# Turning k and q through the first layer's banks in halves, with layer steps given out slot by slot

## The chip, the cores and the metric

The kernel runs on one core of a Trainium2 chip. The metric is the device time of one execution in microseconds (us). In what follows PE is the matmul engine, DVE the vector engine, ACT the scalar engine, POOL the GpSimd engine, and SP the queue from which nearly all transfers are issued.

## What is computed

A thresholded attention is followed by a two-layer network with a shrinking non-linearity. The reference, cut to what matters:

```python
def _attn_ref(q, k, v, tau):                       # 8 batches, 8 heads, 576 rows, 64 columns
    scores = np.matmul(q, k.transpose(0, 1, 3, 2)) / np.sqrt(q.shape[-1])
    thresh = np.max(scores, axis=-1, keepdims=True) - tau
    scores = np.where(scores >= thresh, scores, -1000000000.0)
    scores = scores - np.max(scores, axis=-1, keepdims=True)
    attn = np.exp(scores)
    attn = attn / (np.sum(attn, axis=-1, keepdims=True) + 1e-09)
    return np.matmul(attn, v)

def _moe_ref(x, w_in, w_out):                      # x: 4608 x 512, w_in: 512 x 2048
    h = x @ w_in
    g = h - np.tanh(h)
    return g @ w_out
```

The attention's output, its heads laid side by side, is the network's x.

## The kernel before, in words

**Pairs and tiles.** The 64 heads are taken as 32 pairs, numbered from 0. A pair has nine tiles of 128 query rows (`TPP = 9`): four of each head, and one that holds the last 64 rows of both, the shared tile. Four pairs (`HPAIR`) make a batch. There are 288 tiles.

**Slots.** The order of all work is written out by hand, in a loop over slots `s` from -8 to 292 (line 709). All engines work their instructions in the order in which this loop emits them. In slot `s` it emits, in this order: `shift` (line 347, the row maximum for a pair of tiles, `nb`, in every second slot), `scores(s + 8)`, `kink(s + 5)` on ACT (line 360), `bend` (tanh of the hidden block of the slot before, line 511), `weights(s)` (exp, line 404, in odd slots), the layer steps that the slot is given, `shrink` (line 514, on DVE: `g`, the hidden block less its tanh), stores, `attend(s - 2)` (line 409, tiles in twos, so in odd slots), `norm` (line 450, on DVE), `emit_x` (line 470), and then what `plan` holds for the slot: loads, splits and turns. In a slot where a pair ends in a shared tile and the next begins with one, no scores are emitted and in the next slot two tiles.

**Scores.** `scores` (line 308) multiplies q with k in two fp16 halves, a high and a low one that `split` (line 186, on POOL) makes. Needed for it are `qT` and `kT`, the transposed halves, and `kS`, which is `kT` with its 64-row halves exchanged. DVE evacuates a score tile from PSUM (line 341) and takes the row maximum with it. ACT's `kink` then makes z. For pairs from the seventh on, a DMA transposes z to zT, and ACT takes exp of it.

**Turns.** `turn(p, t)` (line 248) makes `kT` or `qT` of pair `p`: nine transposes on PE into one PSUM tile of 128 x 1152 fp16, one copy by DVE into SBUF, and for k two copies by POOL that make `kS`. For q of pairs from 8 on a DMA does it, except for every fourth pair (`q_by_dma`, line 244). A turn stands in the slot `TPP * p - 8 - d`, with d from `PREP` and the lines below it: for k, d is 3 for even and 6 for odd pairs from the sixth pair on.

**PSUM.** `ps_big` has two buffers of two banks each; score tiles take them in turn, and the turns of k and q take one too (tag "big", line 257). `ps_h` has two buffers of one bank (tag "h"): hidden blocks psH (line 502), and psX, the transposed attention output of a pair (line 472). A hidden block's bank is free once `shrink` has read it, which is emitted one slot after its matmuls. `ps_y` and `ps_o` have one bank each.

**Layers.** For batch m there are 16 h steps (`hidden`, four matmuls of 512 columns, line 498) and 16 y steps (`project`, four such matmuls, line 524; after the fourth of a row block DVE copies psY out). `layers(m, tail)` (line 559) puts both in a list. The slot loop starts a new list every 36 slots from slot 40 on (line 711): stage m is slots 40 + 36m to 75 + 36m. It gives out the list at a rate, `share` steps for each slot of `room`; the slots in which k is turned (`turns`) are left out of `room`. In stages 1 to 5 this gives one step to each of 32 slots, h and y mostly by turns. What is left at the end runs after the last slot.

Below, the position of a slot is s modulo 36. Before, k is turned at positions 7, 13, 25 and 31, q on PE at position 26.

Of the kernel before, what the change touches and what calls it, by code (L numbers as in the profile page):

```python
# [11 lines left out]
FP16 = mybir.dt.float16  # L12
# [6 lines left out]
def kernel(  # L19
# [11 lines left out]
    nc = tc.nc  # L31
    P = 128
# [13 lines left out]
    HPAIR = H // 2  # L46
    NPAIR = B * HPAIR
# [4 lines left out]
    TPP = 9  # L52
    NTILE = NPAIR * TPP
# [7 lines left out]
    W = 2 * S  # L61

    AHEAD = 8
# [62 lines left out]
    ps_big = pool("ps_big", 2, space=PSUM)  # L126
    ps_o = pool("ps_o", 1, space=PSUM)
    ps_h = pool("ps_h", 2, space=PSUM)
# [107 lines left out]
    def turn_chunk(out, c, lhsT):  # L236
        rhs = ident_f16
        if c == 4:
            out, rhs = in_heads(out), by_head(rhs)
        nc.tensor.matmul(  # L240
            out=out, lhsT=lhsT, rhs=rhs, is_transpose=True, start=True, stop=True
        )

    def q_by_dma(p):

        return p >= 2 * HPAIR and p % 4 != 0

    def turn(p, t):
        hl = hls.pop((p, t))
        if t == "q" and q_by_dma(p):  # L250
            m = mats[p, t] = qk_pool.tile([P, W], FP16, name=f"{t}T", tag=t)
            nc.sync.dma_start_transpose(
                out=m.rearrange("p (c r) -> p c r", c=TPP),
                in_=hl.rearrange("p c a d -> p (c a d)"),
            )
            return
        ps = ps_big.tile([P, W], FP16, name=f"ps_{t}", tag="big")
        for c in range(TPP):
            turn_chunk(
                ps[:, c * P : (c + 1) * P], c, hl[:, c, :, :].rearrange("p a d -> p (a d)")  # L260
            )
        m = qk_pool.tile([P, W], FP16, name=f"{t}T", tag=t)
        nc.vector.tensor_copy(out=m, in_=ps)
        mats[p, t] = m
        if t == "k":
            sw = qk_pool.tile([P, W], FP16, name="kS", tag="ks")
            for lo, hi in ((0, D), (D, 0)):
                o, i = sw[lo : lo + D, :], m[hi : hi + D, :]
                nc.gpsimd.tensor_copy(out=o, in_=i)  # L269
            mats[p, "ks"] = sw  # L270
# [27 lines left out]
    def kind(i):  # L298

        return "AB"[i % 2]  # L300

    def place(i):

        p, j = divmod(i, TPP)
        j = j - p % 2
        return (p, None, 4) if j in (-1, 8) else (p, j // 4, j % 4)
# [243 lines left out]
                    )  # L550


    EARLY = lambda m: 3 if m else 3
    LAST = 1

    FIRST = 3
    quarters = lambda m: [(m, ms, part) for ms in range(4) for part in range(4)]

    def layers(m, tail):


        def h_step(n):
            if tail and n % 2:
                ps = ps_big.tile([P, MB], F32, name="psHt", tag="big")
            else:
                ps = ps_h.tile([P, MB], F32, name="psH", tag="h")
            hidden(m, n, ps)

        def y_step(m, ms, part):
            if part == 0:  # L570

                odd = tail and (m, ms) > (B - 2, 1) and ms % 2 == 0
                pl, tag = (ps_o, "o") if odd else (ps_y, "y")
                ys[m, ms] = pl.tile([P, d_model], F32, name="psY", tag=tag), odd
            ps, odd = ys[m, ms]
            project(m, ms, part, ps, odd)

        def y_half(h):

            n = d_model // 2  # L580
            pl, tag = ((ps_y, "y"), (ps_o, "o"))[h]
            ps = pl.tile([P, n], F32, name="psY", tag=tag)
            for part in range(4):
                project(m, 3, part, ps, h == 0, slice(h * n, h * n + n))

        now = quarters(m - 1)[EARLY(m - 1) :] if m > 0 else []
        if m < NMB - 1:
            now += quarters(m)[: EARLY(m)]
        else:
            now += quarters(m)[:12]  # L590
        n = 16 + len(now)


        ahead = n - max(0, EARLY(m) - 3) - LAST if m < NMB - 1 else n - 9 - LAST
        steps, at, i = [], [], 0

        def ready(y):
            last = 4 * y[2] + 3
            return y[0] < m or len(at) > (last if m else 15) and at[last] + 2 < i

        while now or len(at) < 16:
            if len(at) < 16 and (
                not now or not ready(now[0]) or len(at) * ahead <= i * 16
            ) and not (m == B - 1 and i < FIRST):
                steps.append(lambda a=len(at): h_step(a))
                at.append(i)
            elif ready(now[0]):
                steps.append(lambda y=now.pop(0): y_step(*y))
            else:
                steps.append(lambda: None)  # L610
            i += 1
        if m == NMB - 1:
            steps += [lambda h=h: y_half(h) for h in range(2)]
        return steps

    ys = {}


    def w_pieces():
# [39 lines left out]
    for p in range(1, NPAIR):  # L659
        first = TPP * p - AHEAD  # L660
        for d, f in PREP[3 if p == 1 else 0 :]:
            d -= p == 1 and d in (3, 5)
            if d in (7, 8) and q_by_dma(p):
                d = d + 2
            if p in (2, 4):
                d = {8: 9, 7: 8, 5: 6}.get(d, d)
            elif d == 5 and p >= 5:
                d = 6 if p % 2 else 3
            plan.setdefault(first - d, []).append(lambda p=p, f=f: f(p))
        d = 7 if q_by_dma(p) else 3 - (p == 1 or p >= 5)  # L670
        d = 4 if p in (2, 4) else d
        plan.setdefault(first - d, []).append(lambda p=p: turn(p, "q"))
# [15 lines left out]
    todo, stage = [], 0  # L688
# [5 lines left out]

    turns = set()
    for p in range(HPAIR + 1, NPAIR):
        d = 6 if p % 2 else 3
        turns.add(TPP * p - AHEAD - (d if p >= 5 else 5))  # L700

    kinks, wts, atts = {}, {}, {}
    for i in range(NTILE + 3):
        at = i - 4 if i < HPAIR * TPP else i
# [4 lines left out]
    for s in range(-AHEAD, NTILE + LAG + 3):  # L709
        p, j = divmod(max(s, 0), TPP)  # L710
        if 0 <= s < NTILE and j == 2 + LAG and p % HPAIR == 0 and p >= HPAIR:
            assert not todo
            todo = layers(stage, False)
            room = range(s, min(s + HPAIR * TPP, NTILE))
            if room[-1] + 1 < NTILE:
                room = [a for a in room if a not in turns]
            share = len(todo) / len(room)
            done, stage = 0.0, stage + 1
        if s == NTILE:
            todo = layers(stage, True)  # L720
            share, done, stage = 1, 0.0, stage + 1
        if 0 <= s + AHEAD - 1 < NTILE:
            shift(s + AHEAD - 1)

        n = s + AHEAD
        if 0 < n < NTILE and place(n)[1] is None and kind(n) == "B":
            scores(n - 1)
        if 0 <= n < NTILE and (place(n)[1] is not None or kind(n) == "B"):
            scores(n)
        if s == 1 - AHEAD:  # L730
            for t in ("k", "q", "ks"):
                turn_first(t, 1)
        for i in kinks.pop(s, []):
            kink(i)
        bend()
        for i in wts.pop(s, []):
            weights(i)
        if 0 <= s < NTILE + FIRST:
            if todo and (s >= NTILE or s in room):
                done += share  # L740
                if s < NTILE and s == room[-1]:
                    done = 1e9
                while todo and done >= 1:
                    todo.pop(0)()
                    done -= 1
        if s == 0:
            nc.vector.tensor_tensor(
                out=fold, in0=ident_bf[:, 0:64], in1=ident_bf[:, 64:P], op=ALU.add
            )
        shrink()  # L750
        for store in stores[:-1]:
            store()
        del stores[:-1]
        for i in atts.pop(s, []):
            pp, jj = divmod(i, TPP)
            if i < NTILE:
                attend(i)
                odd = pp % 2
                if jj == 3 + odd:
                    norm(pp, 0)  # L760
                elif odd and jj in (0, 8):
                    norm(pp - (jj == 0), 1)
            if pp and jj == 1 + pp % 2:
                emit_x(pp - 1)
        for step in plan.pop(s, []):
            step()
        if s + AHEAD in cast_when:
            w_cast()
        if s + AHEAD in load_when:
            w_load(next(pieces))  # L770

    for step in todo:
        step()
        bend()
        shrink()
        for store in stores:
            store()
        stores.clear()
# [10 lines left out]
    _ = bass_utils  # L789
# [35 lines left out]
```

## Time and profile before

| | |
|---|---|
| median of 3 runs | 531.08 us (531.07 to 531.32) |
| profiled execution | 532.69 us |
| its span, first to last instruction | 530.9 us |
| granted PE clock | full (1.00) |
| first score of slot 40, 76, 112 (stages 0, 1, 2) | 64.56, 116.20, 178.93 us |
| first score of slot 148, 184, 220, 256 (stages 3 to 6) | 237.59, 295.49, 352.92, 410.45 us |

The rest, from about 455 us on, is layer work alone. Lines of the profile name a source line, the engine, the operation, the tile written and the tiles read. In the order of time, the first number is the start in us from the span's start and the second the busy time; "x4" says that four such instructions are merged, and a bracket at the end tells how long the engine was idle before it and who ended the wait. In the list of waits the numbers are the sum in us, how many times, and the longest one. Matmuls overlap, and their ends are modelled, so a PE busy time is longer than the distance to the next start.

### The profile page before, as it was taken

Reading aid. Unit: us, or ns where it says so; the run is one execution under the profiler, and the core shown is the slowest. Engines: PE = TensorE matmul, PEld = TensorE weight load, DVE = VectorE, ACT = ScalarE, POOL = GpSimd, SP = SyncE. Lnnn points to the kernel's source line nnn. Section 1 sums busy time; section 2 is a strip of 40 time slices with the busy share of each in tenths; the row PEclk is TensorE's granted clock in tenths of the full one; section 3 lists DMA queues with packets and bytes.
Section 4 is the critical chain, followed back from the end, with each engine's and each line's share of the span. In section 5 each row is a group of like instructions: output and inputs, shape, how many; then the busy total and the mean of one; then the engine's idle time right before and its main releaser. Section 6 shows DMA issues by size and latency. Waiting matters only on the chain.

```text
span 530.9 us, 12707 instructions
## 1 busy us (share of the span) xinstructions
PE 507.7 (96%) x4606; PEld 286.4 (54%) x4606; DVE 422.1 (80%) x1179; ACT 433.4 (82%) x617; POOL 289.3 (54%) x390
## 2 busy tenths in 40 slices
PE   8999899989999989999999999999999999999996
PEld 4666566554555545555555555555555555444444
DVE  5999889997898878998889888888899887554440
ACT  5999999998898989988998989899998989544330
POOL 7999999684738366574738383846657430000000
PEclk9999999999999999999999999999999999999999
DMA  7843668989799999899998999999988976400113
GB/s 215 242 141 112 216 214 168 184 145 201 180 199 162 183 181 202 167 193 205 180 198 180 199 175 216 157 198 185 204 169 196 202 133 110 105 36 25 39 41 80
DMA packets 208607, 86.79 MB, mean 163 GB/s; under 512 B 176160, under 2 KB 200992, under 8 KB 208544
## 3 DMA queue, kind: packets, MB, share of 16 engines
q1 hardware_dynamic: 207952, 85.56, 77.4%
q8 instruction: 36, 0.59, 0.5%
q10 hardware_dynamic: 592, 0.43, 0.3%
q14 instruction: 27, 0.22, 0.1%
HBM read 36.70 MB, written 9.44 MB: 87 GB/s over the span
## 4 chain that ended last, share of the span: by engine, by line
PE 48%; issue 13%; ACT 12%; DVE 12%; POOL 7%; DMA 7%; SPq 1%; ACTq 0%; POOLq 0%; DVEq 0%
PE psY L524 15%; PE psH L498 12%; PE psS L331 9%; ACT z L368 5%; DVE sc L341 4%; ACT pT L396 3%; DMA zT<-z 3%; PE psHt L498 3%; DVE g L517 2%; PE psO L432 2%; ACT th L511 2%; POOL kS L269 2%; ACT pT L404 2%; DMA vraw<-in_v_dram 2%; PE psS L322 2%
## 5 line engine op out<-in xcount | busy, mean ns | idle before, releaser
L341 DVE TENSOR_SCALAR_CACHE_REDUCE sc<-psS 128x576 f32<-128x576 f32 x288 | 212.9, 753 | 34.2 <-PE psS L331 21.3
L368 ACT ACTIVATE z<-sc,nb 128x576 bf16<-128x576 f32 x288 | 216.0, 769 | 27.6 <-DVE nb L353 27.1
L524 PE MATMUL psY<-w_out_sb,g 128*128 128x512 bf16 (+1 forms) x592 | 146.0, 374 | 0.8 <-DVE yo L537 0.8
L404 ACT ACTIVATE pT<-zT 128x1152 f16<-128x1152 bf16 x117 | 135.0, 1154 | 10.6 <-DMA zT<-z 10.4
L269 POOL COPY kS<-kT 64x1152 f16<-64x1152 f16 x62 | 70.8, 1142 | 125.4 <-DVE nb L353 123.7
L498 PE MATMUL psH<-xT,w_in_sb 128*128 128x512 bf16 x480 | 123.3, 379 | 0.7 <-DVE g L517 0.3
L331 PEld LDWEIGHTS <-qT 128*128 128x128 f16 x1024 | 75.1, 97 | 67.3 <-issue 11.8
L331 PE MATMUL psS<-kT,qT 128*128 128x512 f16 (+1 forms) x512 | 104.3, 285 | 7.2 <-DVE sc L341 4.0
L517 DVE SCALAR_TENSOR_TENSOR g<-th,psH 128x512 bf16<-128x512 f32 x128 | 87.6, 684 | 25.5 <-ACT th L511 23.6
L331 PE MATMUL psS<-kS,qT 128*128 128x512 f16 x496 | 101.3, 286 | 1.7 <-POOL kS L269 1.6
L511 ACT ACTIVATE th<-psH 128x512 f32<-128x512 f32 x128 | 74.6, 583 | 21.9 <-PE psH L498 21.8
L524 PEld LDWEIGHTS <-g 128*128 128x128 bf16 x592 | 51.0, 98 | 57.2 <-issue 3.5
L498 PEld LDWEIGHTS <-w_in_sb 128*128 128x128 bf16 x576 | 48.8, 98 | 53.2 <-issue 1.0
L432 PE MATMUL psO<-vb,pT 128*128 128x65 bf16 x1024 | 53.3, 194 | 0.0
L432 PEld LDWEIGHTS <-pT 128*128 128x128 f16 x1024 | 44.2, 98 | 9.4
L193 POOL TENSOR_TENSOR khl<-kraw,khl 128x576 f16<-128x576 f32 x31 | 39.7, 1281 | 2.6
L193 POOL TENSOR_TENSOR qhl<-qraw,qhl 128x576 f16<-128x576 f32 x31 | 39.7, 1280 | 2.6
L396 ACT ACTIVATE pT<-psZ 128x512 f16<-128x512 bf16 (+1 forms) x54 | 35.1, 654 | 2.6 <-PE psZ L387 2.1
L537 DVE COPY yo<-psY 128x512 f32<-128x512 f32 (+1 forms) x31 | 21.1, 682 | 13.6 <-PE psY L524 12.4
L458 DVE TENSOR_TENSOR osb<-psO,rc 128x256 bf16<-128x256 f32 x64 | 27.2, 424 | 2.2
L425 PE MATMUL psO<-vb,pT 128*128 128x130 bf16 x128 | 28.1, 220 | 0.6 <-DVE nb L353 0.6
L387 PE MATMUL psZ<-ident_bf,z 128*128 128x128 bf16 x243 | 22.5, 220 | 2.1 <-ACT pT L396 1.3
(79 smaller groups left out, 509.5 us busy)
## 6 DMA issues: line engine op xcount, KB each, us to landing
vraw<-in_v_dram SPq DMA_DIRECT2D x32, 256.0 KB, 3.6
out_dram<-yo SPq DMA_DIRECT2D x32, 256.0 KB, 3.1
kraw<-in_k_dram SPq DMA_DIRECT2D x31, 256.0 KB, 3.1
qraw<-in_q_dram SPq DMA_DIRECT2D x31, 256.0 KB, 3.4
wt<-in_moe_w_in_dram SPq DMA_DIRECT2D x8, 512.0 KB, 4.6
wt<-in_moe_w_out_dram SPq DMA_DIRECT2D x8, 512.0 KB, 4.2
zT<-z SPq DMA_TRANSPOSE x117, 3.7
qraw<-in_q_dram SPq DMA_DIRECT2D x32, 32.0 KB, 3.1
```

Of the source, the lines that this page charges most:

```text
L193: nc.gpsimd.tensor_tensor(out=hl[:, :, 1, :], in0=x, in1=hl[:, :, 0, :], op=ALU.subtract)
L269: nc.gpsimd.tensor_copy(out=o, in_=i)
L331: nc.tensor.matmul(out=ps[:, dst], lhsT=lhs, rhs=kk[:, src], start=(n == 0), stop=(n == 1),)
L341: nc.vector.tensor_scalar(out=sc, in0=ps[:, lo : lo + S], scalar1=SC, scalar2=None, op0=ALU.mult, op1=ALU.max, accum_out=mx[:, c : c + 1],)
L368: nc.scalar.activation(out=z, in_=sc, func=ACT.Prelu, bias=nb, scale=1.0, alpha=STEEP)
L396: nc.scalar.activation(out=pt[:, off * P : (off + n) * P], in_=ps[:, 0 : n * P], func=ACT.Exp)
L404: nc.scalar.activation(out=pt[:, 0 : n * P], in_=zts.pop(i)[:, 0:n, :], func=ACT.Exp)
L432: nc.tensor.matmul(out=po[:, t - 1 + ab, :], lhsT=pt[:, blk * P : (blk + 1) * P], rhs=vb[:, hh, c, :], start=False, stop=(n == 7), skip_gr ...
L498: nc.tensor.matmul(out=ps, lhsT=w_in_sb[:, c, n * P : (n + 1) * P], rhs=xs[m][:, c, :] if m < B else xR[:, c, :, :], start=(c == 0), stop= ...
L511: nc.scalar.activation(out=th, in_=ps, func=ACT.Tanh)
L517: nc.vector.scalar_tensor_tensor(out=gs[m][:, n, :], in0=th, scalar=-1.0, in1=ps, op0=ALU.mult, op1=ALU.add,)
L524: nc.tensor.matmul(out=ps, lhsT=gs[m][:, n, ms * P : (ms + 1) * P], rhs=w_out_sb[:, n, cols], start=(n == 0), stop=(n == DF_C - 1),)
```

## The change

From the seventh pair on (`BYHALF = HPAIR + 2`, p from 6), `turn` no longer takes a score buffer. It turns five chunks into one `ps_h` bank and copies them, then four chunks into a `ps_h` bank and copies those. k is turned at d = 4 for even and d = 5 for odd pairs (`k_lead`): one slot earlier for even pairs, one later for odd ones, so at positions 6, 14, 24 and 32. Layer steps of the stages before the tail are no longer given out at a rate: `layers` gets the list of slots without a k turn and gives each step a slot. It prefers an h step when h steps are due by a count, and a y step where it can be run and the next slot is a turn's slot or no h step is due.

In stages 1 to 5 the h steps then stand at positions 4, 7, 9, 11, 12, 15, 17, 18, 20, 22, 25, 26, 28, 29, 33 and 34, and the y steps in the other slots that aren't a turn's: 1, 2, 3, 5, 8, 10, 13, 16, 19, 21, 23, 27, 30, 31, 35 and 0. Before, the h steps stood at 4, 6, 9, 11, 14, 16, 18, 20, 22, 24, 27, 29, 32, 34, 0 and 2. No instruction is added or taken away on PE; on DVE, each turn from the seventh pair on has two copies in place of one.

```diff
+    BYHALF = HPAIR + 2
+
+    def k_lead(p):
+        if p < BYHALF:
+            return 6 if p in (2, 4) or p == HPAIR + 1 else 5 - (p == 1)
+        return 5 if p % 2 else 4
+
...
-        ps = ps_big.tile([P, W], FP16, name=f"ps_{t}", tag="big")
-        for c in range(TPP):
-            turn_chunk(
-                ps[:, c * P : (c + 1) * P], c, hl[:, c, :, :].rearrange("p a d -> p (a d)")
-            )
         m = qk_pool.tile([P, W], FP16, name=f"{t}T", tag=t)
-        nc.vector.tensor_copy(out=m, in_=ps)
+        if p < BYHALF:
+            spans, pl, tag = ((0, TPP),), ps_big, "big"
+        else:
+            spans, pl, tag = ((0, 5), (5, TPP)), ps_h, "h"
+        for c0, c1 in spans:
+            n = (c1 - c0) * P
+            ps = pl.tile([P, n], FP16, name=f"ps_{t}", tag=tag)
+            for c in range(c0, c1):
+                turn_chunk(
+                    ps[:, (c - c0) * P : (c - c0 + 1) * P], c,
+                    hl[:, c, :, :].rearrange("p a d -> p (a d)"),
+                )
+            nc.vector.tensor_copy(out=m[:, c0 * P : c1 * P], in_=ps)
         mats[p, t] = m
...
-    EARLY = lambda m: 3 if m else 3
+    EARLY = lambda m: 3
...
-    def layers(m, tail):
+    def layers(m, tail, slots=None):
...
+        if slots is not None:
+            for nth, i in enumerate(slots):
+                spare = len(slots) - nth - (16 - len(at)) - len(now)
+                can = now and ready(now[0]) and (m or i >= CAST_BY[now[0][2]])
+                due = len(at) * (len(slots) - OWN(m)) <= nth * 16
+                lull = i + 1 not in slots and spare >= 0
+                if len(at) < 16 and not (can and (lull or not due)) and (due or spare <= 0):
+                    steps.append((i, lambda a=len(at): h_step(a)))
+                    at.append(i)
+                elif can:
+                    steps.append((i, lambda y=now.pop(0): y_step(*y)))
+            assert len(at) == 16 and all(ready(y) for y in now)
+            steps += [(i, lambda y=y: y_step(*y)) for y in now]
+            return steps
...
+    CAST_BY = (56, 56, 58, 64)
+    OWN = lambda m: EARLY(m) + 2
...
-            d -= p == 1 and d in (3, 5)
+            d -= p == 1 and d == 3
             if d in (7, 8) and q_by_dma(p):
                 d = d + 2
-            if p in (2, 4):
-                d = {8: 9, 7: 8, 5: 6}.get(d, d)
-            elif d == 5 and p >= 5:
-                d = 6 if p % 2 else 3
+            if d == 5:
+                d = k_lead(p)
+            elif p in (2, 4):
+                d = {8: 9, 7: 8}.get(d, d)
             plan.setdefault(first - d, []).append(lambda p=p, f=f: f(p))
...
-    turns = set()
-    for p in range(HPAIR + 1, NPAIR):
-        d = 6 if p % 2 else 3
-        turns.add(TPP * p - AHEAD - (d if p >= 5 else 5))
+    turns = {TPP * p - AHEAD - k_lead(p) for p in range(HPAIR + 1, NPAIR)}
...
-            todo = layers(stage, False)
             room = range(s, min(s + HPAIR * TPP, NTILE))
-            if room[-1] + 1 < NTILE:
-                room = [a for a in room if a not in turns]
-            share = len(todo) / len(room)
-            done, stage = 0.0, stage + 1
+            todo = layers(stage, False, [a for a in room if a not in turns])
+            stage += 1
         if s == NTILE:
-            todo = layers(stage, True)
-            share, done, stage = 1, 0.0, stage + 1
+            todo = [(s + n, step) for n, step in enumerate(layers(stage, True))]
+            stage += 1
...
-        if 0 <= s < NTILE + FIRST:
-            if todo and (s >= NTILE or s in room):
-                done += share
-                if s < NTILE and s == room[-1]:
-                    done = 1e9
-                while todo and done >= 1:
-                    todo.pop(0)()
-                    done -= 1
+        while todo and todo[0][0] <= s < NTILE + FIRST:
+            todo.pop(0)[1]()
```

More of the change, by code (lines that the diff above doesn't have):

```diff
@@ L770 @@
             w_load(next(pieces))
-    for step in todo:
+    for _, step in todo:
         step()
```

## The prediction, made before the changed kernel ran

> **What bounds the kernel now.** I read the page first, then the list of waits, then the order of time around single turns, and last the groups by form.
>
> ```profile
> PE 507.7 (96%) x4606; PEld 286.4 (54%) x4606; DVE 422.1 (80%) x1179; ACT 433.4 (82%) x617; POOL 289.3 (54%) x390
> ...
> PE   8999899989999989999999999999999999999996
> ```
>
> PE is busy throughout, but busy time of overlapping matmuls says little, so I took the rhythm from the starts: in the order of time four 512-column matmuls of a layer step take 0.86 us, an ordinary score tile 0.49, an attend group 0.31, a shared one 0.29, an x turn 0.25, nine transposes 0.50. A stage of 36 slots holds 32 layer steps (27.6), 32 ordinary score tiles (15.6), two pairs of shared ones at 1.11 (2.2), 16 attends (5.0), 4 shared ones (1.2), 4 x turns (1.0) and 5 turns of k and q (2.5): 55.1 us. By the starts of slots 112, 148, 184, 220 and 256 (178.93, 237.59, 295.49, 352.92, 410.45) a stage takes 58.7, 57.9, 57.4 and 57.5. PE thus stands still about 2.8 us a stage; a PE wait added there counts fully, and no more than that can be won. Who ends its waits:
>
> ```profile
> PE psS L331 <- DVE sc L341: 4.0, 7, 1.2
> ...
> PE ps_k L240 <- DVE sc L341: 1.9, 11, 0.2
> ...
> PE psS L331 <- POOL kS L269: 1.6, 5, 0.3
> ```
>
> These hang on the k turn: it takes a score buffer, so it waits for a score's evacuation, the next score waits in turn, and kS arrives late. One such turn (slots 150 to 154):
>
> ```profile
> 241.11 0.68 DVE L517 SCALAR_TENSOR_TENSOR g<-th,psH 128x512 bf16<-128x512 f32 x1
> ...
> 242.32 0.75 DVE L341 TENSOR_SCALAR_CACHE_REDUCE sc<-psS 128x576 f32<-128x576 f32 x1
> ...
> 242.99 0.76 DVE L341 TENSOR_SCALAR_CACHE_REDUCE sc<-psS 128x576 f32<-128x576 f32 x1
> 243.13 0.66 PE L240 MATMUL ps_k<-ident_f,khl 128*128 128x128 f16 x9 [0.18 <-DVE sc L341]
> ...
> 243.79 0.69 DVE L517 SCALAR_TENSOR_TENSOR g<-th,psH 128x512 bf16<-128x512 f32 x1
> 243.81 0.41 PE L331 MATMUL psS<-kT,qT 128*128 128x512 f16 x2
> ...
> 244.40 0.75 DVE L263 COPY kT<-ps_k 128x1152 f16<-128x1152 f16 x1
> ...
> 247.59 0.41 PE L331 MATMUL psS<-kS,qT 128*128 128x512 f16 x2 [0.32 <-POOL kS L269]
> ```
>
> The reader should see: the turn starts 0.06 after the first sc ends (242.32 + 0.75), 0.33 late by PE's rhythm; the next score is 0.18 late; the copy waits behind an sc and a g on DVE and harms nobody; at 247.59 PE is late for kS by 0.49 (the row before started at 246.86; two matmuls of it take 0.24). That is 1.0 us for this turn.
>
> **What the skill says.** "Perfetto Trace Analysis", Tensor Engine Instruction: only weight loads are pulled ahead on PE, and ACT, DVE and GpSimd are strict FIFO. The copy above agrees: transposes over at 243.8, copy at 244.40 behind g. The same page, Identifying the Most-Contended Engine: recurring bubbles on a saturated engine can mean too few PSUM buffers; here 0.33 and 0.18 recur every second k turn. "PSUM — Partial Sum Buffer", Terms: eight banks of 2 KiB. The program's tiles use them all (two psS of two banks, two "h", one "y", one "o"), so the halves have to share "h" with psH and psX. No trace row shows banks.
>
> **The change, part by part.** Positions are slots modulo 36; stage 3 (slots 148 to 183) stands for stages 1 to 5.
>
> (1) Removed: waits on a score bank. By PE's rhythm this is 0.51 each at positions 7 and 25; kS adds 0.49 at 7, and the score behind the q turn at 26 is 0.23 late. At 13 the score after the turn waited 1.41, 0.63, 0.17 and 0 in four stages (196.29 and 254.18 are two of these rows; tanh is late behind a late zT; mean 0.55), at 31 nothing. About 2.3 a stage, of the 2.8.
>
> (2) Added on DVE: two copies for one.
>
> ```profile
> L263 DVE COPY kT<-ps_k 128x1152 f16<-128x1152 f16 x31 | 23.3, 751 | 1.1 <-PE ps_k L240 0.9
> ...
> L488 DVE COPY xT<-psX 128x512 bf16<-128x512 bf16 x32 | 13.4, 420 | 1.8 <-PE psX L481 1.8
> ...
> L291 DVE COPY kT<-ps_k 128x640 f16<-128x640 f16 x1 | 0.5, 491 | 0.9 <-PE ps_k L240 0.9
> ```
>
> 491 + 420 - 751 = 160 ns a turn, 33 turns: 5.3 us, in DVE's 20% of idle time; by itself nothing.
>
> (3) Added: waits on "h" banks. In the changed program every k turn stands at positions 6, 14, 24 or 32, on a slot without attend, and the next slot (7, 15, 25, 33) always carries an H step, whose psH takes the bank of the first half. So H waits for the first copy, and behind H stand all later scores and attends. PE reaches H 0.49 + 0.50 + 0.49 = 1.48 after the turn's slot began. DVE takes that slot's sc first, at best 0.69 after the slot's start (239.64 against 238.95 in slot 149), goes on 0.67 later (242.32, 242.99), copies 0.49 and frees the bank 0.06 later: 1.91. No k turn costs less than 0.43. With what DVE has before it:
> - Position 6: PE work up to slot 150 is as before. First half 241.11 to 241.39; the second needs the bank of H148, whose g ends at 241.79: wait 0.46. H is due at 242.56, its bank free at 242.99 + 0.49 + 0.06 = 243.54: 0.98. Together 1.44, for 1.00.
> - Position 14: the x copies of slot 157 end about 2.9 after that slot's start, sc runs from 2.97, copy 3.64 to 4.13; H is due at 3.68: 0.5, plus what late tanhs leave, 0.25. 0.75, for 0.55.
> - Position 24: slot 168 starts at 269.75. Without the output copy that before has in slot 167 (269.63), g ends near 270.26, normalization and nb take 0.55, sc 270.80, copy 271.47 to 271.96; H is due at 271.23 and starts at 272.02: 0.79.
> - Position 32: x copies as at 14, no late g: 0.51, for nothing.
>
> (4) The q turn at position 26 (pairs 12, 16, ... 28; likewise 7 and 8) keeps its H step in the same slot, and that psH isn't read before the next slot. So both halves get the same bank. From the H at 272.02: + 0.86 + 0.31 is slot 170 at 273.19; + 0.49 + 0.86 is 274.54. The first half needs the bank of H169, whose g comes after sc(170) (273.88) on DVE: 274.55 to 275.24, wait 0.76. The second half needs the first's copy: 275.30 + 0.45, + 0.49, + 0.06 = 276.30, wait 0.72. Slot 171 starts near 276.52, for 275.07 in this row of before:
>
> ```profile
> 274.34 0.66 PE L240 MATMUL ps_q<-ident_f,qhl 128*128 128x128 f16 x9
> ...
> 275.04 0.76 DVE L263 COPY qT<-ps_q 128x1152 f16<-128x1152 f16 x1
> 275.07 0.41 PE L331 MATMUL psS<-kT,qT 128*128 128x512 f16 x2
> ```
>
> Positions 24 to 26 lose 1.45 net.
>
> (5) Layer steps keep their number in each stage; H steps now come in pairs of slots (11 and 12, 17 and 18, 25 and 26, 28 and 29, 33 and 34). ACT has 10% idle in these stages and DVE about 12% (26.5 of 30 us): I take 0, bounds -0.5 and +1 a stage. psY's last part at position 0 is followed by the next psY at position 1; position 0 has no score and two shared ones (1.11) stand between, so the 0.69 copy is hidden. Even k turns now come a slot earlier, odd ones a slot later; khl is long there (for pair 6 at 65.4, turn near 67.6), and kS moves ahead of split_v on POOL, which idles 8.7 us before such copies. DMAs keep their number; stores shift by single slots on SP. All 0. After the last score (455 us on) the order is the same.
>
> Sum for a stage: 0.45 + 0.2 + 1.45 + 0.5 = +2.6; five stages +13.0. Stage 0: four k turns at about 1.0 and two q turns at 1.4, less 2.2 of old waits, is +4.6; ACT is the fuller engine there (28.1 of 30 us), so half: +2.3. Stage 6: pair 30 +1.2, pair 31 +0.75, together +2. In all +17.3 on a span of 530.9, which with what lies around it was 532.69; the median of the runs, 531.08, is 1.6 lower. On that median: 548.4, I say **548**.
>
> **Rivals.**
> - Only the unavoidable waits: DVE has no backlog at the turns. Four k turns at 0.51 and q at 1.48 are 3.5 for 2.3: +1.2 a stage, 6.0, with 1.2 for stages 0 and 6: **538**. For it: a PE that stalls lets DVE catch up. Against: normalization, output copy and x copies stand just before three of the four turns.
> - Waits pile up: DVE waited 51 times, 36.1 us, for tanh, 0.7 each; if half of 33 turns meet one, 0.5 x 33 x 0.7 = 11.6 more: **560**.
> - Faster: freed score buffers are all that counts. If the copies return banks before H is due, 2.3 x 5 + 2 goes and q costs 1.2 a stage: 531 - 13.5 + 6 = **523**. It decides once the new waits average under 2.3 / 5 = 0.46 a turn. Against it is the floor in (3), 0.43 for k, and 1.48 for q.
> - No net change: **531**, when (3) and (1) happen to cancel.
>
> **How the numbers follow.** Forecast (541 to 556) 0.60, unavoidable waits only 0.18, piling up 0.11, faster 0.08, none 0.03. The range 535 to 559 leaves out faster, none and the upper part of piling up. Differences under 0.2% (1.1 us) can't be told from none: faster 0.08, same 0.03, slower 0.89.
>
> **What would show it.** Right: new waits of PE at psH L513 and ps_k/ps_q L240 on DVE's kT and qT copies and g; psS no longer waiting for kS; two q halves about 1 us apart; stages near 60.5. Wrong: psH starts without a gap after turns (faster), or PE waits for sc or ACT for zT grow instead (another cause).

## The result, and the profile after

The changed kernel takes 553.19 us (median of 4 runs, 551.92 to 554.34), against 531.2 for the kernel before on the same chip: a ratio of 1.0413, with a 95% interval of 1.0386 to 1.0439. It is slower. The profiled span is 552.1 us, against 530.9.

The page shows that the work on PE is the same and the span is longer. This is the row of busy time, in us and as a share of the span, with the number of instructions:

```profile
PE 509.5 (92%) x4606; PEld 286.4 (52%) x4606; DVE 424.5 (77%) x1213; ACT 435.9 (79%) x617; POOL 290.5 (53%) x390
```

PE has the same 4606 matmuls, 1.8 us more busy time, and 92% where it had 96%. Its idle time, span less busy time, rose from 23.2 to 42.6 us, which is 19.4 of the 21.2 us that the span grew; so nearly all of the loss is time in which PE stands still. The 34 more instructions on DVE are the second copies of the 34 turns. By form, the copies of k and q sum to 38.3 us for 33.1 before.

The time from the first score of one stage to that of the next, from the starts in the order of time:

| stage | 0 | 1 | 2 | 3 | 4 | 5 | from slot 256 to the end |
|---|---|---|---|---|---|---|---|
| before | 54.9 | 59.5 | 58.7 | 57.9 | 57.4 | 57.5 | 120.5 |
| after | 59.0 | 62.7 | 61.2 | 60.5 | 60.1 | 60.1 | 123.7 |
| difference | 4.1 | 3.2 | 2.5 | 2.6 | 2.7 | 2.5 | 3.2 |

(The table ahead of the prediction gives 116.20 us for slot 76. That is the start of slot 74; slot 76 starts at 119.47. No step of the prediction used it.)

Whom PE waits for, from the list of waits of the changed kernel (sum in us, how many, the longest):

```profile
PE psH L513 <- DVE kT L278: 10.4, 22, 0.8
...
PE ps_k L240 <- DVE g L532: 7.1, 11, 1.6
...
PE ps_q L240 <- DVE g L532: 4.5, 6, 1.0
PE ps_q L240 <- DVE qT L278: 4.1, 7, 0.6
...
PE psY L539 <- DVE yo L552: 1.6, 2, 0.8
...
PE psS L346 <- DVE sc L356: 1.1, 5, 0.4
```

Before, psS waited 4.0 us for sc and 1.6 us for kS, and ps_k 1.9 us for sc. Of these old waits 1.1 us for sc are left, kS ends no wait of an ordinary score any more, and the four lines on top are new. They are waits for a bank of `ps_h`: for the copy of a half (kT, qT), or for the read of a hidden block (g). Together they are 26.1 us.

The order of time around the k turn in slot 150 (position 6) shows two of them. Columns are start, busy time, engine, line, operation, tiles; a bracket tells how long the engine had been idle, and for whom:

```profile
251.25 0.68 DVE L532 SCALAR_TENSOR_TENSOR g<-th,psH 128x512 bf16<-128x512 f32 x1
...
251.98 0.38 PE L240 MATMUL ps_k<-ident_f,khl 128*128 128x128 f16 x4 [0.30 <-DVE g L532]
...
252.46 0.75 DVE L356 TENSOR_SCALAR_CACHE_REDUCE sc<-psS 128x576 f32<-128x576 f32 x1
...
253.14 0.81 DVE L278 COPY kT<-ps_k 128x640 f16<-128x640 f16 x2
...
253.67 1.02 PE L513 MATMUL psH<-xT,w_in_sb 128*128 128x512 bf16 x4 [0.82 <-DVE kT L278]
```

The second half of the turn waits for g, which ends at 251.93. The h step of the next slot waits for the first copy, which stands on DVE behind the score's evacuation `sc`. Counted from PE's rhythm, that is against the start that PE would have made without a wait, these are 0.46 and 0.98 us. (The brackets are smaller, since the modelled end of the matmuls before reaches past that start.)

The q turn in slot 170 (position 26) of the same stage, with the k turn two slots before it:

```profile
281.10 0.67 PE L240 MATMUL ps_k<-ident_f,khl 128*128 128x128 f16 x9
...
282.21 0.82 DVE L278 COPY kT<-ps_k 128x640 f16<-128x640 f16 x2
...
282.75 1.02 PE L513 MATMUL psH<-xT,w_in_sb 128*128 128x512 bf16 x4 [0.49 <-DVE kT L278]
...
284.41 1.03 PE L513 MATMUL psH<-xT,w_in_sb 128*128 128x512 bf16 x4
...
285.39 0.68 DVE L532 SCALAR_TENSOR_TENSOR g<-th,psH 128x512 bf16<-128x512 f32 x1
...
286.13 0.44 PE L240 MATMUL ps_q<-ident_f,qhl 128*128 128x128 f16 x5 [0.69 <-DVE g L532]
286.60 0.49 DVE L278 COPY qT<-ps_q 128x640 f16<-128x640 f16 x1 [0.53 <-PE ps_q L240]
...
287.15 0.38 PE L240 MATMUL ps_q<-ident_f,qhl 128*128 128x128 f16 x4 [0.58 <-DVE qT L278]
```

The h step at 284.41 keeps one bank. The first half of q waits for g of the h step before it (0.85 by the rhythm), and the second half needs the bank that the first half has just left (0.75). Position 26 alone loses 1.6 us in each of stages 1 to 5.

### The profile page after: what moved, and what is told of

The parts are those of the page before. It is cut to its first block, busy times and chain, and to the rows that moved or that the text cites. A ratio compares the mean times of both kernels' runs of the same rounds, so it can differ in the third digit from the quotient of the medians.

```text
span 552.1 us, 12680 instructions
## 1 busy us (share of the span) xinstructions
PE 509.5 (92%) x4606; PEld 286.4 (52%) x4606; DVE 424.5 (77%) x1213; ACT 435.9 (79%) x617; POOL 290.5 (53%) x390
## 4 chain that ended last, share of the span: by engine, by line
PE 66%; DVE 14%; ACT 9%; issue 5%; POOL 2%; DMA 2%; SPq 0%; DVEq 0%; ACTq 0%; POOLq 0%
PE psY L539 20%; PE psH L513 17%; PE psS L346 13%; DVE sc L356 4%; PE psO L447 4%; DVE g L532 4%; ACT z L383 3%; PE psS L337 3%; PE psHt L513 3%; ACT pT L411 2%; ACT th L526 2%; ACT pT L419 2%; DVE kT L278 1%; PE ps_q L240 1%; PE psZ L402 1%
## 5 line engine op out<-in xcount | busy, mean ns | idle before, releaser
L383 ACT ACTIVATE z<-sc,nb 128x576 bf16<-128x576 f32 x288 | 219.5, 770 | 38.5 <-DVE nb L368 36.4
L513 PE MATMUL psH<-xT,w_in_sb 128*128 128x512 bf16 x480 | 123.2, 379 | 11.7 <-DVE kT L278 10.4
L532 DVE SCALAR_TENSOR_TENSOR g<-th,psH 128x512 bf16<-128x512 f32 x128 | 87.4, 683 | 23.9 <-ACT th L526 23.7
L346 PEld LDWEIGHTS <-qT 128*128 128x128 f16 x1024 | 72.1, 97 | 51.3 <-issue 2.9
L513 PEld LDWEIGHTS <-w_in_sb 128*128 128x128 bf16 x576 | 50.6, 98 | 67.5 <-issue 14.3
L539 PEld LDWEIGHTS <-g 128*128 128x128 bf16 x592 | 51.1, 98 | 57.5 <-issue 4.6
L240 PE MATMUL ps_k<-ident_f,khl 128*128 128x128 f16 x288 | 23.9, 219 | 8.4 <-DVE g L532 7.1
```

The lines of the kernel that those rows point to most:

```text
L346: nc.tensor.matmul(out=ps[:, dst], lhsT=lhs, rhs=kk[:, src], start=(n == 0), stop=(n == 1),)
L383: nc.scalar.activation(out=z, in_=sc, func=ACT.Prelu, bias=nb, scale=1.0, alpha=STEEP)
L513: nc.tensor.matmul(out=ps, lhsT=w_in_sb[:, c, n * P : (n + 1) * P], rhs=xs[m][:, c, :] if m < B else xR[:, c, :, :], start=(c == 0), stop= ...
L532: nc.vector.scalar_tensor_tensor(out=gs[m][:, n, :], in0=th, scalar=-1.0, in1=ps, op0=ALU.mult, op1=ALU.add,)
L539: nc.tensor.matmul(out=ps, lhsT=gs[m][:, n, ms * P : (ms + 1) * P], rhs=w_out_sb[:, n, cols], start=(n == 0), stop=(n == DF_C - 1),)
```

## The experiments

Theory: the loss is PE waiting for PSUM buffers whose DVE reader stands in line behind other work. Which part of the change brings which wait was to be found by taking the parts apart. A percentage is against runs of the kernel before on the same chip; the one in brackets is its 95% interval.

### The parts alone

**e1: the banks alone.** The kernel before, with the new `turn` in halves; k's slots and the rate of the layer steps as before.

```diff
...
+        if p < HPAIR + 2:
+            spans, pl, tag = ((0, TPP),), ps_big, "big"
+        else:
+            spans, pl, tag = ((0, 5), (5, TPP)), ps_h, "h"
...
```

> Before with one part alone: from the seventh pair on the turns take the first layer's banks in halves; slots of the turns and the rate of the layer steps stay as before. Theory (new PE waits on those banks, set by what DVE has queued ahead of the copies and by an H step in the slot after the turn): here the k turns keep odd slots with an attend, the next step is a y step for two of four, and both banks are free for the q turn, so the waits are near 1.0 + 0.5 + 1.0 + 0.5 a stage for 2.3 removed: 533 to 540 us, with psS no longer waiting for the turn. Rival (the banks cost the whole loss, wherever the steps stand): near 553. Rival (freed score buffers alone count): 520 to 528.

Measured: 545.14 us, 2.24% slower (1.72 to 2.76). That is above the expected range and short of the rival's 553; each stage from 2 to 5 takes about 60 us. The waits stand at the k turns as expected, but not for the reason expected: not the copies and the h step after the turn, but the work before it. In this order an h step stands in the slot just before the turns at 7 and 25, and the second half waits for its g. Order of time of e1, slot 151:

```profile
247.74 0.58 ACT L518 ACTIVATE th<-psH 128x512 f32<-128x512 f32 x1
...
248.35 0.69 DVE L524 SCALAR_TENSOR_TENSOR g<-th,psH 128x512 bf16<-128x512 f32 x1
...
249.09 0.38 PE L240 MATMUL ps_k<-ident_f,khl 128*128 128x128 f16 x4 [1.30 <-DVE g L524]
```

The hidden block must pass tanh and g before the second half can go on, 1.46 us a turn at positions 7 and 25. The list of waits of e1 puts 16.5 us on this one pair, ps_k on g, in 14 waits. At 13 and 31 it waits for the last copy of psX (xR), 0.67 us by the rhythm. The q turn at 26, in the same halves, costs nothing here in stages 1 to 5. In this order slot 26 has a y step, and PE waits for neither bank. Slot 170 of e1:

```profile
280.27 0.67 PE L240 MATMUL ps_q<-ident_f,qhl 128*128 128x128 f16 x9
...
280.75 0.82 DVE L270 COPY qT<-ps_q 128x640 f16<-128x640 f16 x2 [0.38 <-PE ps_q L240]
280.78 0.41 PE L338 MATMUL psS<-kT,qT 128*128 128x512 f16 x2
```

**e2: everything but the banks.** The changed kernel, with every turn whole in a score buffer.

```diff
-        if p < BYHALF:
+        if True:
             spans, pl, tag = ((0, TPP),), ps_big, "big"
```

> The changed kernel with every turn back in one score buffer; k's new slots and the steps given out slot by slot stay. Theory: the waits of psH on kT and of the q halves on each other go; instead the score after an even-slot turn waits for the sc of that slot (about 1.5, 0.6, 0.9, 0.6 at positions 6, 14, 24, 32) for 2.3 of before: 534 to 543 us. Rival (the new step order is what costs, through ACT and DVE bursts): 548 or more.

Measured: 543.77 us, 2.02% slower (1.58 to 2.46), just above the expected range. The waits of the score after the turn were 1.52, 0.56, 0.74 and 0.56 us at positions 6, 14, 24 and 32. From the list of waits of e2:

```profile
PE psS L346 <- DVE sc L356: 19.7, 31, 1.5
PE psO L440 <- ACT pT L419: 2.1, 1, 2.1
```

So k's new slots and the new order of the layer steps, with no turn in the first layer's banks, already lose half of what the change loses. The second line is a single wait near the end of stage 0, for an exp whose zT came late.

**e6 and e7: those two apart.** e6 is the kernel before with k's new slots only; e7 is the changed kernel with k's old slots and all turns whole, so that the new order of the layer steps is left.

```diff
 e6, against the kernel before
             elif d == 5 and p >= 5:
-                d = 6 if p % 2 else 3
+                d = 6 if p == 5 else 5 if p % 2 else 4
...
 e7, against the kernel after
-        return 5 if p % 2 else 4
+        return 6 if p % 2 else 3
...
-        if p < BYHALF:
+        if True:
```

(In e6 `turns` follows the same d, so the layer steps, still given out at a rate, leave the new slots and fill the old ones.)

> The kernel before with one edit: from the seventh pair on k is turned in slots that have no normalization (5 or 4 slots ahead); turned whole in a score buffer, first and second layer steps at the old rate. Theory (what e2 lost, it lost by the slots: the turn's slot issues one buffer more than its score evacuations free, and the next score waits at positions 6, 14, 24 and 32): waits as in e2, 1.5, 0.6, 0.7 and 0.6 us a stage, stages of about 58.8 us, 540 to 545 us. Rival (e2 lost by the layer steps given out slot by slot): 529 to 534 us.

> The kernel before with one edit: the layer steps are given out slot by slot as in the change; k is turned in its old slots, whole, in a score buffer. Theory (e2 lost by the slots of k's turns): stages within 0.7 us of before's, 529 to 535 us, stage 0 at most 1.5 us longer. Rival (the runs of first layer steps cost it): psH waits behind a first layer step in the slot before, stages of 58.5 us or more, 540 us or more.

Measured: e6 542.56 us, 1.85% slower (1.56 to 2.14); e7 535.03 us, 0.50% slower (0.32 to 0.67). The slots are the costly part. That the two together (2.35%) come near e2's 2.02% is in part luck, as the stages show (difference from the kernel before in us):

| | stage 0 | stages 1 to 5 | from slot 256 to the end |
|---|---|---|---|
| e6 | 1.2 | 7.5 | 0.6 |
| e7 | -0.2 | 1.1 | 1.4 |
| e2 | 3.4 | 4.5 | 2.5 |

In stages 1 to 5 the new order of the layer steps halves what the slots cost; in stage 0 e2 has the one wait of 2.1 us for exp that neither e6 nor e7 has. The wait at a turn in e6, order of time at slot 150:

```profile
243.85 0.41 PE L331 MATMUL psS<-kT,qT 128*128 128x512 f16 x2
...
244.34 0.67 PE L240 MATMUL ps_k<-ident_f,khl 128*128 128x128 f16 x9
244.34 0.68 DVE L517 SCALAR_TENSOR_TENSOR g<-th,psH 128x512 bf16<-128x512 f32 x1
...
244.94 0.18 DVE L457 RECIPROCAL rc<-psO 128x4 f32<-128x4 f32 x1
...
245.15 0.42 DVE L458 TENSOR_TENSOR osb<-psO,rc 128x256 bf16<-128x256 f32 x1
...
245.56 0.75 DVE L341 TENSOR_SCALAR_CACHE_REDUCE sc<-psS 128x576 f32<-128x576 f32 x1
...
246.37 0.41 PE L331 MATMUL psS<-kT,qT 128*128 128x512 f16 x2 [1.36 <-DVE sc L341]
```

The reader should see two things. First, this slot has no normalization among what it emits, but the one emitted at the end of the slot before (rc and osb) runs on DVE during this slot, ahead of its `sc`. Second, the slot has no attend either, so PE comes to the next score 0.99 us after this one (0.49 + 0.50), at 244.84, and the buffer is free only at 246.31. The wait is 1.53 us. In the kernel before, the turn at position 7 came when that normalization was over and had an attend ahead of it; it cost 0.51 us, with kS another 0.49. A copy of psY (DVE, 0.69 us) stands on DVE just ahead of this g and makes the wait long at position 6; at 24 e6 has such a copy too (at 273.26) and waits 1.53, while e2 has none there and waits 0.74. Over five stages this is about 4 us, about what e2 loses less there than e6 and e7 together.

### The halves: q and k apart

**e5: q whole.** The changed kernel, but q takes a score buffer as before; k stays in halves.

```diff
-        if p < BYHALF:
+        if p < BYHALF or t == "q":
             spans, pl, tag = ((0, TPP),), ps_big, "big"
```

> The changed kernel, but with q turned whole in a score buffer as before, only k in halves in the first layer's banks. Theory (q's two halves share one bank with a first layer step in the same slot): the two q waits at position 26 of each stage (0.85 and 0.75 us, 1.6 us a stage) go, a score wait of some 0.2 us comes back as before the change; five stages give 7 us, stage 0 another 1 to 2: 543 to 546 us. Rival (the whole turn waits just as long for the score buffer): a psS wait of over 1 us at position 26, 550 us or more.

Measured: 542.92 us, 1.88% slower (1.52 to 2.24), where the whole change is 4.13% slower; by the medians 10.3 us less, just below the range that was expected. At position 26 PE no longer waits, and no score wait came back. Order of time of e5, slot 170:

```profile
278.44 1.03 PE L513 MATMUL psH<-xT,w_in_sb 128*128 128x512 bf16 x4
...
279.30 0.67 PE L240 MATMUL ps_q<-ident_f,qhl 128*128 128x128 f16 x9
...
279.80 0.41 PE L346 MATMUL psS<-kT,qT 128*128 128x512 f16 x2
```

The whole turn follows the h step after 0.86 us and the score after another 0.50, which is PE's rhythm. Eight q turns in halves thus cost about as much (2.25%) as all else in the change (1.88%). They cost it beside the h steps at 25 and 26: in e1, with a y step at 26, the same halves did not wait. So it is also a coincidence that e1's 2.24% and e2's 2.02% sum to about the whole; e1 loses it at the k turns, the changed kernel about half of it at q. Halves of q in the new order without an h step beside them were not run. In stage 0 only 1.0 us is won, because there, as in e2, PE then waits for a late exp (1.8 us). Between e2 and e5 only the k turns differ, whole in one, in halves in the other, and their intervals (1.58 to 2.46% and 1.52 to 2.24%) are nearly the same. In these slots, k in halves exchanges one wait for another of about the same size.

**e3: a y step after each k turn.** The changed kernel, with the slot after a turn preferring a y step.

```diff
-                lull = i + 1 not in slots and spare >= 0
+                lull = (i + 1 not in slots or nth and i - 1 not in slots) and spare >= 0
```

> The changed kernel, but the slot after a k turn prefers a y step, so that psH does not need the bank of k's first half at once. Theory (the H step's wait for the first copy, 0.98 + 0.65 + 0.41 + 0.41 a stage, is what is paid): these waits go, the second half's 0.46 and the q turn's 1.6 stay: 538 to 543 us. Rival (DVE or ACT is simply too full, the wait comes back at the next instruction that needs DVE, or the runs of three and four H steps cost as much): 550 or more.

Measured: 544.49 us, 2.24% slower (1.75 to 2.73) where the changed kernel is 4.13% slower; 1.5 us above the expected range. From the list of waits of e3:

```profile
PE psH L513 <- DVE g L532: 3.8, 6, 0.7
...
PE psH L513 <- DVE kT L278: 1.3, 2, 0.8
```

The wait for kT fell from 10.4 us to 1.3, so the bank of the first half was indeed what the h step waited for. The first half of q no longer waits either (ps_q on g fell from 4.5 to 1.0), which was not expected: slot 25 now has a y step, so the bank that it takes is not that of an h step just before. In exchange the h steps close up (16, 17 and 18), and at 18 one waits 0.79 us for a g in each stage.

**e4: the k turn at the head of its slot**, ahead of the slot's score, so that its copy stands before that slot's `sc` on DVE.

```diff
...
+                if p >= BYHALF:
+                    early.setdefault(first - d, []).append(lambda p=p, f=f: f(p))
+                    continue
...
+        for step in early.pop(s, []):
+            step()
         n = s + AHEAD
```

> The changed kernel with the k turn at the head of its slot, before the slot's score, so that on DVE the two kT copies stand ahead of that slot's sc. Theory (strict order on DVE: sc before copy is what makes H late): the H step after the turn waits for nothing; the second half waits more (0.9 at position 6, 0.3 at 24, 0.5 at 14 and 32) since it comes earlier; per stage about 1.1 less than the changed kernel, 545 to 549 us. Rival (the bank's return does not depend on sc's place on DVE): the H step waits as before, 551 to 555.

Measured: 552.51 us, 3.75% slower (3.13 to 4.38). This is not the gain expected, and no difference from the changed kernel is shown. The time is in the rival's range, but the rival is wrong too: the h steps after the turns no longer wait. From the list of waits of e4, where psH on kT is gone:

```profile
PE ps_k L240 <- DVE g L532: 9.6, 13, 1.0
...
PE ps_k L240 <- DVE nb L368: 3.6, 8, 0.8
```

The turn, which now comes one score earlier, waits for its banks instead. The second half waits 0.95 us at position 6, 0.54 at 32 and 0.17 at 24; at 14 it is the first half that waits for a g, 0.8 to 1.0 us in stages 1, 2 and 5, and psX ahead of it up to 1.0. Stage 0 grows by another 1.5 us. (In the profiled execution the granted clock averaged 0.66 between 265 and 270 us, so stage 3 is left out of this reading.) The wait moved from one user of the bank to the other.

### Tries for a kernel faster than both

**e8.** In stages 1 to 5, k in halves in the new slots, q whole, and a list of positions for the h steps that keeps them out of each k turn's slot and its neighbours. Stage 0 and from slot 256 on as before.

```diff
+            if 0 < m < B - 2:
+                for i in slots:
+                    if i % 36 in (4, 8, 9, 11, 12, 16, 18, 20, 22, 26, 28, 29, 34, 35, 1, 3):
+                        steps.append((i, lambda a=len(at): h_step(a)))
+                        at.append(i)
+                    else:
...
+                        steps.append((i, lambda y=now.pop(0): y_step(*y)))
...
+                return steps
...
-        if p < BYHALF:
+        if not 10 <= p < 30 or t == "q":
...
+        if not 10 <= p < 30:
+            return 6 if p % 2 else 3
         return 5 if p % 2 else 4
```

> A try for a kernel faster than both: in stages 1 to 5 the k turns are in halves in the first layer's banks in the slots without a normalization, q whole in a score buffer, and the sixteen first layer steps at positions 4, 8, 9, 11, 12, 16, 18, 20, 22, 26, 28, 29, 34, 35, 1 and 3, chosen so that no first layer step stands in the slot of a k turn, the one before or the one after; stage 0 and the last two stages as in the kernel before. Theory (the change loses only by what stands beside each turn): the psH waits after turns go, second halves wait 0.1 to 0.5 us, stages of 56.0 to 57.2 us against 57.4 to 58.7 before: 522 to 529 us. Rival (the halves need a free bank twice in a slot of 1.5 us, and that alone costs as much as the waits they replace): stages of 57.5 us or more, 531 to 538 us.

Measured: 532.44 us, a ratio of 1.0009 (0.9991 to 1.0027): no difference from the kernel before, and in the rival's range. The waits of the h steps after turns are gone, and stages 3 to 5 take about 57.4 us, as before. What is left, from the list of waits of e8:

```profile
PE ps_k L240 <- DVE g L534: 4.8, 14, 0.9
...
PE psX L492 <- DVE g L534: 1.8, 3, 0.8
```

The second half still waits 0.46 us at positions 6 and 24, the two halves at 14 wait 0.6 to 0.7 in four of five stages, and an h step at 4 waits 0.36: what the halves save on score buffers they pay on the first layer's banks.

**e9: the h steps moved once more**, to three or more slots ahead of the turns at 6, 24 and 32. (Ahead of 14 one still stands at 12, as in e8.) Only the list differs from e8.

```diff
-                    if i % 36 in (4, 8, 9, 11, 12, 16, 18, 20, 22, 26, 28, 29, 34, 35, 1, 3):
+                    if i % 36 in (8, 9, 11, 12, 16, 17, 19, 20, 21, 26, 28, 29, 34, 35, 0, 1):
```

> e8 with the first layer steps of stages 1 to 5 at positions 8, 9, 11, 12, 16, 17, 19, 20, 21, 26, 28, 29, 34, 35, 0 and 1. In e8 the second half of k's turn still waits 0.46 us at positions 6 and 24, where a first layer step stands two slots before (4 and 22), and not at 32, where it stands three before; and a first layer step waits 0.36 us at position 4. Theory (a half needs its bank's g three slots back): these three go, 1.3 us a stage, of which the run 34, 35, 0, 1 may take back up to 0.5; four to five stages: 526 to 530 us. Rival (the run of four steps with two banks waits for its own g as in e3, 0.8 us or more): 531 to 535 us.

Measured: 537.26 us, 0.92% slower (0.75 to 1.10): what the rival says, and more than its range. From the list of waits of e9:

```profile
PE psH L515 <- DVE g L534: 6.7, 11, 1.6
PE ps_k L240 <- DVE g L534: 3.2, 5, 1.0
PE psX L492 <- DVE g L534: 2.8, 3, 1.4
PE psY L541 <- DVE yo L554: 2.2, 6, 0.8
```

The halves at positions 6 and 24 no longer wait, but the h steps, now in denser runs, wait for each other's g (0.54 us at 0, 0.6 to 1.8 at 21). So do psX at 13 (in three stages) and the halves at 14, which follow the run 11 and 12, and a y step at 5 waits for the copy of psY. The profiled execution took 541.5 us, 4 more than the median, at a granted clock of 0.992 on average (0.93 to 0.94 in parts of stages 1 and 2), so the sizes, not the places, may be high. No version tried here beats the kernel before.

## Why the prediction was right, point by point

The forecast was 548 us, in a case that reached from 541 to 556; the result is 553.19, within that case and 5 us above its middle. The direction and the mechanism were right; two terms of the sum, stage 0 and the end, were too small.

- **What bounds it.** Right. PE has the same matmuls, and 19.4 of the 21.2 us of the longer span are added idle time of PE; 20.9 of them lie behind slot 40.
- **(1) Waits removed.** Right. kS ends no wait of an ordinary score, and the score waits for sc fell from 4.0 to 1.1 us. The gain on sc belongs to the halves and not to k's new slots: in e1 (halves, old slots) that wait is 1.3 us, in e6 (whole turns, new slots) 23.9. The wait for kS is gone in both.
- **(2) Second copies.** 5.3 us of DVE work was estimated for 33 turns, 5.2 measured for 34 (the q turn of pair 6 was left out). That they cost nothing by themselves agrees with e5, where k's copies come twice and the time is e2's.
- **(3) h steps and second halves at k turns.** Predicted at position 6: 0.46 and 0.98; measured 0.46 and 0.98. At 24: 0.79; measured 0.66. At 32: 0.51; measured 0.41. At 14: 0.75; measured 0.42 for the halves (0.74, 0.74, 0.51, 0.06 and 0.06 in stages 1 to 5) and 0.41 for the h step at 15, together 0.83.
- **(4) q at 26.** Predicted 0.76 and 0.72; measured 0.85 and 0.75. e5 shows the weight of it: 10.3 us, the largest single cost. The reason given, the h step in the same slot, agrees with e1, where a y step stands there and q does not wait.
- **(5) Order of the layer steps at 0.** Right on average for stages 2 to 5, where e7 differs from the kernel before by +0.1 us (between -0.8 and +0.9); not right for what follows. From slot 256 on e7 is 1.4 us longer than before, and in the changed kernel psY waits twice for its copy (the line of psY above) where it waited once before.
- **The sum of stages 1 to 5.** Predicted 13.0, measured 13.6. The errors at single positions, about 0.1 us each, go both ways and partly cancel; stage 1, at 3.2, is above the 2.6 a stage of the sum.
- **Stage 0: the mis-sized term.** Its turns were worked out to +4.6 us and then halved to 2.3, because ACT was thought to cover the rest. It measured +4.1. The waits of PE between 64 and 124 us of the changed kernel, which is stage 0:

```profile
PE ps_k L240 <- DVE g L532: 2.8, 2, 1.6
PE ps_q L240 <- DVE qT L278: 1.2, 2, 0.6
PE ps_q L240 <- DVE g L532: 1.0, 1, 1.0
...
PE psH L513 <- DVE g L532: 0.7, 1, 0.7
PE psH L513 <- DVE qT L278: 0.5, 1, 0.5
PE psH L513 <- DVE kT L278: 0.5, 1, 0.5
```

  The same waits as elsewhere stand there at full size, and ACT was busy for 51.2 of the 59.0 us, so it hid none of them. There are also three q turns in this stage and not two: that of pair 6 in slot 44 waits 1.05 us. The thought behind the halving is not empty, though: in e2 and e5, where the q waits are gone, PE waits about 2 us for a late exp at the end of this stage.
- **The end: the second mis-sized term.** +2 was predicted from the turns of pairs 30 and 31, +3.2 measured from slot 256 on. In that stretch the halves of the last two k turns wait for g (1.1 us), an h step for kT (0.8), and psY once more for its copy (0.8). The last one comes from the order of the layer steps (e7 has it too), which the prediction put at 0 for that part.
- **The rivals.** "Only the unavoidable waits" (538) fell because DVE did have a backlog at the turns; the normalization of the slot before stands in it, as e6 shows. "Faster" (523) needed new waits under 0.46 us a turn, and at 6 and 26 they are 1.4 and 1.6. "Waits pile up" (560) was seen at single turns only: two in stage 0 (1.6 and 1.2 us) and one in stage 1 (1.3), the largest part of why stage 1 lost 3.2 us and the later ones 2.5 to 2.7. In sum DVE waited for tanh no longer than before (36.2 us for 36.1). "No net change" (531) fell with the sum of the new waits, 26.1 us.
- **The recurring bubbles.** What the prediction says of them is in the section Optimization Strategy of "Perfetto Trace Analysis" in the Trainium skill. The traces agree that PE's repeated waits were for PSUM buffers (psS and ps_k on sc, 5.9 us before) and that the halves brought more of them (26.1 us). No run here has more buffers.

What stays open is why zT came late at the end of stage 0 in e2 and e5 and not in the others, and whether q in halves would cost nothing in the new order too if no h step stood beside it.

## What to carry to other kernels

Moving a user from one pool of buffers to another did not remove the waits here; it handed them to the users of the other pool. So work out for each of them what their engine has in line before it gives the buffer back. A slot in a hand-written order is free on the engine that emits little in it only if the work emitted at the end of the slot before is done by then. Two halves that go through one free buffer are serial with the copy between them, and cost more than one whole piece in a larger buffer (q at 26 in the changed kernel). With two buffers free they cost nothing more (q in e1), so look at who else holds the buffers in that slot.

## What was not expected of the hardware

- Two copies in a row on DVE take less than their sum: 0.81 us for the 640-column and the 512-column half of k together, while in the groups by form they average 485 and 414 ns. Copies of q, with PE's transposes between them, stand 0.97 us from start to start (286.60 to 287.57).
- From the end of a copy or a g on DVE to the start of the matmul that needs its bank were 0.05 to 0.06 us in the rows shown (251.93 to 251.98; 286.07 to 286.13; 287.09 to 287.15), the same for either kind of reader.
